# Sigmoid attention and a gated MLP: the scores' bias as a constant in the instruction

## The chip, the core and the metric

The kernel runs on one core of a Trainium2 chip. Such a core has a matrix engine (TensorE, PE in the profile; its weight loads are listed apart as PEld), three engines for elementwise work (VectorE, DVE; ScalarE, ACT; GpSimd, POOL) and SyncE (SP), which here only issues transfers. All of them run their own instruction streams in order and wait for each other through semaphores. Data moves between the device's memory (HBM), the on-chip SBUF and the matrix engine's accumulators (PSUM); 16 DMA engines carry the transfers. The metric is device time in microseconds; the kernel before takes 382.32 us (median of three runs, 382.04 to 382.57).

## What is computed

Per head, attention with a sigmoid in place of the softmax, and then an MLP over the joined heads:

```
scores = scale * matmul(q, k^T) - log(S)       # scale = 1/sqrt(64), S = 448
attn   = 1 / (1 + exp(-scores))
x      = matmul(attn, v)                       # 8 batches x 12 heads x 448 x 64, joined to 3584 x 768
h      = x @ w_in                              # 3584 x 2048
out    = (h * sigmoid(h)) @ w_out              # 3584 x 768
```

The term -log(S) = -6.1 is one number for the whole kernel. It is added inside the sigmoid's instruction on ScalarE, which computes func(scale * input + bias).

## The kernel before

**Units of scores.** The twelve heads of a batch are worked off in groups of four (`g`, three to a batch, 24 in all). A group's 448 keys are cut into seven chunks of 64, so there are 168 units `(g, ch)`. For each, `scores` (L170) issues four matmuls of 64x64 tiles (L177) that fill a PSUM tile `psc` of two banks, and one sigmoid on ScalarE (L184) that reads 128 x 896 scores from it and writes `attnT` to SBUF as float16. There are two `psc` buffers, so the scores of unit n can start when the sigmoid of unit n-2 has read its buffer. `values` (L194) multiplies `attnT` with v (L208, into two `pav` tiles) and VectorE scales the sum into `xT` (L219).

**Transposes.** Scores need q and k with the head dimension on the partitions. The first groups are transposed on PE (`pe_transpose`, L148) and copied out of PSUM by VectorE or ScalarE (L155, L138); later groups are reordered by ScalarE or VectorE (L138, L163) and transposed by DMA on SP's queue (L164).

**The MLP.** `h_unit` (L230) issues six matmuls for 128 columns of h (L236, into `ph`), a sigmoid on ScalarE (L248, into `tsig`, bias 0.0) and a product on VectorE (L249, into `gTr`). `out_set` (L289) forms two row blocks of the output with seven products in place of eight (L307, into `po`), with VectorE's sums (L315, L319 and on) and one ScalarE copy (L322, `m1`) between them, and stores them through SP's queue (L300). `ph`, `po`, `pav`, the transposes' `ptr` and the filling matmuls' `pw` share four PSUM buffers of one bank.

**What sets the order.** The order on every engine is fixed when the kernel is built, and nothing in it depends on how long an instruction takes. After the transposes of group 0 come 24 units in a loop (L535); behind each unit, a table `behind` (L510) puts filling matmuls on a dummy tile (`keep_busy`, L135), transposes of groups 1 to 3, rounds of `values`, or the first matmuls of the MLP (`begin`, behind units 21 and 23). From unit 24 on, units come in pairs, and `stretch` (L399) issues MLP steps between them up to a budget of nanoseconds written into the code (`paces`, L540).

**Loads.** POOL issues the loads of q, k, v (L78), `w_in` (L108, in four column quarters) and `w_out` (L115) in program order on one queue; they also turn float32 into float16. Each load waits for its buffer to be free and for a slot of the queue.

**The bias.** `bias_s` (L101) is a 128x1 float32 tile. VectorE fills it with -log(S) (L422); a first sigmoid on it (L423, into `warm`) makes ScalarE load its function table early; then L184 reads it as the bias operand 168 times. Small tiles take 32 bytes of each partition. `bias_s` lies at bytes 16768 to 16800, `warm` behind it, and behind that w_in, w_out and all other tiles, each at a multiple of 64 bytes.

Of the kernel before, what the change touches and what calls it, by code (L numbers as in the profile page):

```python
# [11 lines left out]
F32 = mybir.dt.float32  # L12
AF = mybir.ActivationFunctionType
# [4 lines left out]
def kernel(  # L18
# [9 lines left out]
    nc = tc.nc  # L28

    B, H, S, D = q.shape  # L30
    NT, DMODEL = out.shape
    DFF = moe_w_in.shape[1]
    P = 128
# [12 lines left out]
    QKSCALE = 1.0 / math.sqrt(D)  # L46
    NEG_LOG_S = -math.log(S)

    cpool = ctx.enter_context(tc.tile_pool(name="cpool", bufs=1))
# [48 lines left out]
        return st  # L98

    ident = cpool.tile([P, P], F16, tag="ident", name="ident")  # L100
    bias_s = cpool.tile([P, 1], F32, tag="biass", name="bias_s")  # L101
    warm = cpool.tile([P, 1], F32, tag="warm", name="warm")
    w_in_sb = cpool.tile([P, NCC, DFF], F16, tag="w_in_sb", name="w_in_sb")
    w_out_sb = cpool.tile([P, NFC, DMODEL], F16, tag="w_out_sb", name="w_out_sb")
# [63 lines left out]
    attnT = {}  # L168

    def scores(g, ch):  # L170
        attnT[g, ch] = p12.tile([P, 2, S], F16, tag="attnT", name="attnT")
        psc = ps_sc.tile([P, 2, 512], F32, tag="pssc", name="psc")
        for half in range(2):
            own = slice(half * HP, (half + 1) * HP)
            for j in range(2):
                rows = slice(j * D, (j + 1) * D)
                nc.tensor.matmul(  # L177
                    psc[own, j, :S],
                    qkT["k", g][rows, ch, own],
                    qkT["q", g][rows, :, own],  # L180
                    start=True,
                    stop=True,
                )
        nc.scalar.activation(  # L184
            attnT[g, ch], psc[:, :, :S], AF.Sigmoid, bias=bias_s, scale=QKSCALE
        )

    xT = {}
# [230 lines left out]
    load_w_in(0)  # L419

    nc.vector.memset(dummy, 0.5)
    nc.vector.memset(bias_s, NEG_LOG_S)  # L422
    nc.scalar.activation(warm, bias_s, AF.Sigmoid, bias=bias_s, scale=1.0)  # L423
    nc.vector.tensor_copy(flat["q", 0][:, :, :SPLIT], first_q[:, :, :SPLIT])
    act_copy(flat["q", 0][:, :, SPLIT:], first_q[:, :, SPLIT:])

# [108 lines left out]
    for n in range(NT_B + 3):  # L535
        scores(*units[n])
        for do, *what in behind.get(n, ()):
            do(*what)
# [3 lines left out]
    for n in range(NT_B + 3, len(units), 2):  # L542
        burst = units[n : n + 2]
        if n == 2 * NT_B:
            values_if_any()
            stretch(21500)
        for u in burst:
            scores(*u)
        values_if_any()
        rows_if_any()  # L550
        for g, ch in burst:
            if ch == NCH - 1:
                waiting.append(g)
        if n in (24, 30):
            transposes(4 + (n - 24) // 6, "k")
        elif n in (26, 32):
            transposes(4 + (n - 26) // 6, "q")
        stretch(paces[1] if 1 not in ready else paces[n // NT_B])
# [34 lines left out]
```

## Time and profile before

| | |
|---|---|
| runs, median (lowest to highest) | 382.32 us (382.04 to 382.57) |
| profiled execution, first to last instruction | 380.8 us |
| PE busy, share of the span | 372.2 us, 98% |
| ScalarE busy | 240.3 us, 63% |
| VectorE busy | 234.3 us, 62% |
| L184, 168 times | 158.9 us busy, 1010 ns each on average |
| granted TensorE clock | 0.998 on average |
| moved by DMA | 42.80 MB |

The profiled execution's own time is given as its span alone; the runs' times also hold what lies before the first and after the last instruction.

A line of the table of groups reads: source line, engine, operation, tile written<-tiles read, shapes, count | busy us in all, mean ns of one | idle time of the engine just before them, and what ended most of it. A line of the order of time reads: start and length in us, engine, line, operation, tiles, shapes, count, and in brackets the engine's idle time before it with what ended it; like instructions that follow one another are merged. In the chain that ended last, the work is followed back from the last instruction to what released each step. Matmuls overlap in the pipeline of the array, so the length of one in the profile is longer than the step from one to the next.

### The profile page before, as it was taken

The page shows a single profiled execution, that of the slowest core. Times are in us where ns is not written, and L with a number is a line of the kernel's source. Part 1 is how long each engine was busy: PE and PEld are TensorE (multiplying, and loading weights), DVE is VectorE, ACT ScalarE, POOL GpSimd, SP SyncE. Part 2 cuts the span into 40 slices and gives each one's busy share as a digit, 9 for nine tenths or more (in the row PEclk, how much of TensorE's full clock was granted, in tenths as well). Part 3 has the DMA queues.
Part 4 walks back from the last instruction along what each step waited for, and adds up shares of the span by engine and source line. Part 5 has one row for each costly group of instructions (what it writes and reads, how often), then busy time and mean ns, then how long its engine had stood idle before and what let it go on. Part 6 is the DMA issues. An engine that isn't in the chain of part 4 may idle for free.

```text
span 380.8 us, 7666 instructions
## 1 busy us (share of the span) xinstructions
PE 372.2 (98%) x3083; PEld 187.2 (49%) x3083; DVE 234.3 (62%) x416; ACT 240.3 (63%) x329; POOL 92.9 (24%) x158
## 2 busy tenths in 40 slices
PE   7999999999999999999999999999999999999995
PEld 3444445545554445444555444544455444555663
DVE  2446646996565666556767647735857446656773
ACT  4998885858777875778444686577774787044000
POOL 8856325402662323121311303101100000000000
PEclk9999999999999999999999999999999999999999
DMA  7999999994999937937939849535337300110233
GB/s 123 169 171 205 206 203 183 139 143 104 158 243 195 180 50 97 181 44 79 141 80 190 97 112 121 61 96 74 48 79 103 84 3 2 42 43 0 77 91 83
DMA packets 66403, 42.80 MB, mean 112 GB/s; under 512 B 37056, under 2 KB 62912, under 8 KB 66368
## 3 DMA queue, kind: packets, MB, share of 16 engines
q0 software_dynamic: 28032, 22.59, 43.7%
q1 hardware_dynamic: 38112, 19.41, 28.7%
q8 instruction: 24, 0.39, 0.4%
q10 hardware_dynamic: 224, 0.33, 0.3%
q14 instruction: 11, 0.09, 0.1%
HBM read 45.61 MB, written 11.01 MB: 149 GB/s over the span
## 4 chain that ended last, share of the span: by engine, by line
PE 87%; ACT 7%; DVE 3%; issue 1%; DMA 1%; POOL 1%; ACTq 0%; POOLq 0%
PE ph L236 35%; PE po L307 34%; PE psc L177 10%; PE pav L208 8%; ACT attnT L184 5%; DVE gTr L249 1%; DMA kf<-in_k_dram 1%; ACT qr L138 1%; DVE T L278 1%; PE ptrk L148 1%; ACT tsig L248 0%; POOL kf L78 0%; ACT kr L138 0%; PE ptrq L148 0%; DVE S L319 0%
## 5 line engine op out<-in xcount | busy, mean ns | idle before, releaser
L184 ACT ACTIVATE attnT<-psc,bias_s 128x896 f16<-128x896 f32 x168 | 158.9, 1010 | 53.5 <-PE psc L177 53.4
L236 PE MATMUL ph<-xT,w_in_sb 128*128 128x448 f16 x768 | 153.2, 353 | 0.0
L249 DVE TENSOR_TENSOR gTr<-ph,tsig 128x448 f16<-128x448 f32 x128 | 78.1, 623 | 72.0 <-ACT tsig L248 71.4
L236 PEld LDWEIGHTS <-w_in_sb 128*128 128x128 f16 x768 | 71.9, 98 | 75.7 <-issue 12.9
L248 ACT ACTIVATE tsig<-ph 128x448 f16<-128x448 f32 x128 | 68.2, 545 | 47.8 <-PE ph L236 46.2
L78 POOL DMA_DIRECT2D vf<-in_v_dram x48 | 28.6, 613 | 136.6 <-PE pav L208 136.3
L307 PEld LDWEIGHTS <-S 128*128 128x128 f16 x448 | 42.3, 98 | 33.9 <-issue 6.8
L315 DVE SCALAR_TENSOR_TENSOR osb<-po,osb 128x384 f32<-128x384 f32 x70 | 37.7, 555 | 25.1 <-PE po L307 24.5
L177 PE MATMUL psc<-qT,kT 64*64 64x448 f16 x672 | 50.6, 362 | 1.6 <-ACT attnT L184 1.0
L219 DVE TENSOR_SCALAR xT<-pav 128x448 f16<-128x448 f32 x48 | 27.7, 620 | 30.1 <-PE pav L208 30.1
L307 PE MATMUL po<-T,S 128*128 128x384 f16 x224 | 40.6, 327 | 0.1
L307 PEld LDWEIGHTS <-gTr 128*128 128x128 f16 x304 | 28.7, 98 | 23.4 <-issue 5.2
L307 PE MATMUL po<-w_out_sb,S 128*128 128x384 f16 x224 | 39.9, 326 | 0.0
L208 PE MATMUL pav<-attnT,vf 64*64 64x448 f16 x672 | 37.6, 349 | 0.4 <-DVE gTr L249 0.4
L78 POOL DMA_DIRECT2D qf<-in_q_dram x46 | 27.6, 610 | 41.3 <-DVE qr L163 16.9
L307 PE MATMUL po<-w_out_sb,gTr 128*128 128x384 f16 x192 | 34.7, 327 | 0.0
L78 POOL DMA_DIRECT2D kf<-in_k_dram x50 | 30.2, 615 | 7.6 <-DVE kr L163 4.4
L177 PEld LDWEIGHTS <-kT 64*64 64x64 f16 x672 | 14.9, 104 | 32.0 <-issue 30.5
L208 PEld LDWEIGHTS <-vf 64*64 64x64 f16 x672 | 20.1, 107 | 12.4 <-issue 1.8
L315 DVE SCALAR_TENSOR_TENSOR osb<-po,m 128x384 f32<-128x384 f32 x42 | 23.2, 552 | 4.1 <-PE po L307 2.5
L322 ACT ACTIVATE m<-po 128x384 f32<-128x384 f32 x14 | 6.9, 491 | 23.7 <-PE po L307 23.7
L307 PE MATMUL po<-T,gTr 128*128 128x384 f16 x112 | 21.4, 326 | 0.0
(41 smaller groups left out, 132.4 us busy)
## 6 DMA issues: line engine op xcount, KB each, us to landing
out_dram<-osb SPq DMA_DIRECT2D x54, 192.0 KB, 2.9
vf<-in_v_dram POOLq DMA_DIRECT2D x48, 112.0 KB, 4.7
kf<-in_k_dram POOLq DMA_DIRECT2D x46, 112.0 KB, 5.7
qf<-in_q_dram POOLq DMA_DIRECT2D x46, 112.0 KB, 6.0
w_in_sb<-in_moe_w_in_dram POOLq DMA_DIRECT2D x4, 768.0 KB, 10.6
w_out_sb<-in_moe_w_out_dram POOLq DMA_DIRECT2D x4, 768.0 KB, 17.4
kT<-kr SPq DMA_TRANSPOSE x18, 6.0
qT<-qr SPq DMA_TRANSPOSE x18, 5.9
```

What stands on the lines that cost most here:

```text
L78: nc.gpsimd.dma_start(flat[name, g][half * HP : (half + 1) * HP, :, c0:c1].rearrange("p i c d -> p i (c d)"), source[name][b, h0 : h0 + 2] ...
L138: nc.scalar.activation(o, i, AF.Copy)
L177: nc.tensor.matmul(psc[own, j, :S], qkT["k", g][rows, ch, own], qkT["q", g][rows, :, own], start=True, stop=True,)
L184: nc.scalar.activation(attnT[g, ch], psc[:, :, :S], AF.Sigmoid, bias=bias_s, scale=QKSCALE)
L208: nc.tensor.matmul(pav[half][j * D : (j + 1) * D, :S], flat["v", g][own, j, ch, :], at[own, j, :], start=(ch == 0), stop=(ch == NCH - 1),)
L219: nc.vector.tensor_scalar_mul(xT[b][:, half * NQ + iq, :], pav[half][:, :S], SX)
L236: nc.tensor.matmul(ph[:, :S], w_in_sb[:, cc, fc * P : (fc + 1) * P], xT[b][:, cc, :], start=(at == 0), stop=(at == NCC - 1),)
L248: nc.scalar.activation(tsig, ph[:, :S], AF.Sigmoid, bias=0.0, scale=ISX)
L249: nc.vector.tensor_mul(gTr[:, fc, (b % 2) * S : (b % 2) * S + S], ph[:, :S], tsig)
L307: nc.tensor.matmul(po[:, :NO2], a[:, fc, :], w[:, fc, :], start=(fc == 0), stop=(fc == NHC - 1))
L315: nc.vector.scalar_tensor_tensor(out=o, in0=po, scalar=sign, in1=x, op0=ALU.mult, op1=ALU.add)
L322: nc.scalar.activation(m1, po, AF.Copy, scale=ISX)
```

## The change

The tile `bias_s` and its memset are gone. L184 names the number itself as its bias, which then stands in the instruction as L248's 0.0 does. The first sigmoid now reads `warm`, which VectorE sets to zero before, and takes the same constant.

```diff
     ident = cpool.tile([P, P], F16, tag="ident", name="ident")
-    bias_s = cpool.tile([P, 1], F32, tag="biass", name="bias_s")
     warm = cpool.tile([P, 1], F32, tag="warm", name="warm")
...
         nc.scalar.activation(
-            attnT[g, ch], psc[:, :, :S], AF.Sigmoid, bias=bias_s, scale=QKSCALE
+            attnT[g, ch], psc[:, :, :S], AF.Sigmoid, bias=NEG_LOG_S, scale=QKSCALE
         )
...
     nc.vector.memset(dummy, 0.5)
-    nc.vector.memset(bias_s, NEG_LOG_S)
-    nc.scalar.activation(warm, bias_s, AF.Sigmoid, bias=bias_s, scale=1.0)
+    nc.vector.memset(warm, 0.0)
+    nc.scalar.activation(warm, warm, AF.Sigmoid, bias=NEG_LOG_S, scale=1.0)
```

## The prediction

> **What bounds the kernel now.** I read the page first, then the busy time by windows, the waits of PE, and then the order of time around the few moments at which PE stands still. From the page:
>
> ```profile
> span 380.8 us, 7666 instructions
> PE 372.2 (98%) x3083; PEld 187.2 (49%) x3083; DVE 234.3 (62%) x416; ACT 240.3 (63%) x329; POOL 92.9 (24%) x158
> ...
> PE 87%; ACT 7%; DVE 3%; issue 1%; DMA 1%; POOL 1%; ACTq 0%; POOLq 0%
> ...
> L184 ACT ACTIVATE attnT<-psc,bias_s 128x896 f16<-128x896 f32 x168 | 158.9, 1010 | 53.5 <-PE psc L177 53.4
> ...
> L248 ACT ACTIVATE tsig<-ph 128x448 f16<-128x448 f32 x128 | 68.2, 545 | 47.8 <-PE ph L236 46.2
> ...
> L322 ACT ACTIVATE m<-po 128x384 f32<-128x384 f32 x14 | 6.9, 491 | 23.7 <-PE po L307 23.7
> ```
>
> PE is busy for 98% of the span and carries 87% of the chain. The edited instruction, L184, is the largest group on ScalarE (168 of them), but ScalarE is idle 53.5 us in front of it, waiting for scores. A shorter L184 therefore counts only where PE waits for ScalarE. The windows say where that can be; the columns are window, length, PE busy (instructions), granted clock, DMA share, GB/s:
>
> ```profile
> 7.80:16.00 8.20, 7.47 (x90) 1.00 1.20 178
> 16.00:26.30 10.30, 9.42 (x163) 1.00 1.10 154
> 26.30:80.00 53.70, 53.22 (x449) 1.00 1.30 184
> 80.00:331.00 251.00, 250.52 (x2088) 1.00 0.68 103
> ```
>
> Between 26.3 and 331 us PE idles for less than 1 us. Before 26.3 us it has holes, and the DMA engines are full (share above 1). The order of time there, first ScalarE, then PE, then POOL's issues:
>
> ```profile
> 7.81 21.78 ACT L184 ACTIVATE attnT<-psc,bias_s 128x896 f16<-128x896 f32 x24 [0.80 <-PE psc L177]
> ```
>
> ```profile
> 15.92 0.58 PE L148 MATMUL ptrq<-ident,qf 128*64 128x128 f16 x14 [0.38 <-DMA qf<-in_q_dram]
> ...
> 20.24 0.58 PE L148 MATMUL ptrq<-ident,qf 128*64 128x128 f16 x14
> 20.76 0.38 PE L177 MATMUL psc<-qT,kT 64*64 64x448 f16 x4
> ...
> 24.22 0.38 PE L177 MATMUL psc<-qT,kT 64*64 64x448 f16 x4 [0.19 <-ACT attnT L184]
> ...
> 26.33 0.93 PE L236 MATMUL ph<-xT,w_in_sb 128*128 128x448 f16 x4
> ```
>
> ```profile
> 16.07 0.59 POOL L78 DMA_DIRECT2D qf<-in_q_dram  x1 [1.50 <-DMA qf<-in_q_dram]
> 16.65 0.85 POOL L108 DMA_DIRECT2D w_in_sb<-in_moe_w_in_dram  x1
> ```
>
> So for its first 24 units of scores ScalarE runs without a pause, one sigmoid every (21.78 - 1.01)/23 = 0.90 us; PE waits for it, but also for loads.
>
> **The change part by part.** *The instruction.* One immediate-bias sigmoid is in the trace: L248, 545 ns for 448 elements. With L322 (491 ns for 384, no bias) it gives (545-491)/64 = 0.84 ns an element, and a fixed part of 545-373 = 172 ns. L184 has 1007 (its median) less 896 x 0.833 = 747, that is 260. So the tile costs 88 ns and L184 should take some 918. Over 168 of them ScalarE gains 15 us, nearly all of it idle time.
>
> *Back to back.* Two instructions overlap, so what counts in a burst is the period. L184 to L184 is 0.89 at its shortest (starts at 23.11, 24.00 and 24.89 in the chain). For the immediate form this pair of L248 bounds it:
>
> ```profile
> 33.28 0.98 ACT L248 ACTIVATE tsig<-ph 128x448 f16<-128x448 f32 x2
> ```
>
> 0.98 less one duration of 0.54 is a period of 0.43, that is 0.06 above the 0.373 of streaming. For 896 elements: 0.747 + 0.06 = 0.81. The lower bound of the gain is zero (the overlap shrinks by as much as the duration), the upper 0.09; the pair is the same operation from PSUM, so I take 0.805, 0.085 less. The Trainium skill, page "ScalarE: Activation LUTs", section "What ACT_TABLE_LOAD costs", has 186 ns + 0.833 an element with immediates, 93 for each pointer operand, and an overlap of 93. By it the new period would be an estimated 0.84, and the same working gives a sum of some 0.8 instead of 1.15; the trace has a larger overlap (1.007 - 0.89 = 0.117), and it decides.
>
> *The first 26 us.* Unit n (counted from 0) has two score buffers, so its scores start 0.05 us after the sigmoid of unit n-2 ends. Up to 16 us nothing is won: unit 10's scores follow the transposes at 15.92, which wait for a load; a faster ScalarE lets PE arrive earlier and wait longer, some 0.9 us instead of 0.38. Again at 20.24: that q load was issued at 16.07 and took 4.0 us, to 20.07, and unit 15's scores at 20.76 stand behind it. From here ScalarE sets the pace. Scores are ready 0.43 after they start (45.54 to 45.97 in a later unit), so unit 15's sigmoid can start at 21.19 instead of 22.22; today ScalarE is behind by a unit. Unit 19's starts at 21.19 + 4 x 0.805 = 24.41 and ends at 25.33; unit 21's scores start at 25.38 (26.01 before), and L236 follows 0.32 later at 25.70. But L236 reads w_in, issued at 16.65 and 8.9 us on its way, so landed at 25.55; with the 0.17 that PE needed after the q load it starts at 25.72. Before: 26.33. The stage gives 0.61, bounded by 0 (w_in a little later) and by 1.0 (loads earlier).
>
> *Behind it* PE is full, and the next loads have slack: w_in's second quarter lands at 31.7 for a use at 33.3, the third at 38.9 for 42.2; w_out's last at 61.9 for a use at 63.3. So 0.61 stays.
>
> *Three later stalls.* PE waits three times for a buffer that a short ScalarE burst frees:
>
> ```profile
> 34.12 0.77 PE L148 MATMUL ptrq<-ident,qf 128*64 128x128 f16 x14
> ```
>
> ```profile
> 49.02 0.57 PE L208 MATMUL pav<-attnT,vf 64*64 64x448 f16 x8 [0.42 <-DVE gTr L249]
> ```
>
> ```profile
> 144.43 0.38 PE L177 MATMUL psc<-qT,kT 64*64 64x448 f16 x4 [0.48 <-ACT attnT L184]
> ```
>
> The first is 0.77 where others take 0.58. Before the first two, two L184 stand ahead of the tsig that DVE's gTr needs; before the third, two L184 themselves. Each burst shortens by two steps, 0.17 to 0.18, which is less than the stall. Together 0.54; between 0 and, if the stalls went whole, about 1.1.
>
> *The rest.* The memset of bias_s (0.06 us on DVE) gives way to one of warm, and the first sigmoid (294 ns) still runs long before the first data at 4.8 us: nothing, covered by the wait for the first loads. No DMA is added, and POOL, SP and the order on every engine stay. One thing moves: bias_s holds 32 bytes of each partition (16768 to 16800), and every tile allocated after it starts 32 bytes lower, at 32 past a multiple of 64 instead of on one. I cost that at nothing; the trace has no instruction to price it, and it is a rival in both directions.
>
> Sum: 0.61 + 0.54 = 1.15 us off the profiled span of 380.8, so 379.65. The median of the runs, 382.32, is 1.5 above the span, which I take as lying around it: **381.2 us**, 0.3% faster. 0.2% (0.76 us) is about what a measurement of this kernel can tell from no change.
>
> **The rivals.** *Loads eat the first stage.* For it: PE already waits for q at 15.92, and w_in's landing and the faster ScalarE meet within 0.02 us. If w_in is 0.6 late in another execution, only the three stalls are left: 381.8. Against: the runs agree within 0.5 us.
>
> *The price of the bias stays,* because the constant is kept in SBUF or the overlap shrinks: 382.3. Against it stand the 172 ns of L248, whose 0.0 is a constant of the same kind; only a special treatment of zero would speak for it.
>
> *The moved addresses cost PE time.* Place: the 1552 full-array matmuls of L236 and L307, at 189 and 163 ns a step, in stretches where PE never idles. Each ns on one is 1.55 us, so 0.75 ns undoes the gain and 1.25 ns makes it slower by over 0.2%; 2 ns give 384.3. For it: no operand in the trace lies 32 past a multiple of 64. Against: both steps are within 3 ns of streaming alone.
>
> *The moved addresses help the loads.* If transfers move whole 256-byte blocks of SBUF, a row of q, k or v (two runs of 896 bytes) touches 64 pieces of 32 bytes now and 62 then, 3% less; from 6.6 us on, q at 20.07 comes 0.4 earlier and w_in 0.6, so ScalarE's pace decides: 1.0 + 0.54, or 380.8. The Trainium skill, page "DMA: Bandwidth & Descriptors", section "How a descriptor splits into AXI transactions", says that a transaction must begin on a 256 B boundary; no row here shows whether it holds for writes.
>
> **How the numbers follow.** Forecast 0.50 (380.8 to 381.6 by its own bounds), loads eat it 0.18, price stays 0.06, addresses cost PE 0.11, loads helped 0.15. Faster by over 0.2% (below 381.56): forecast and helped loads, 0.65. Within 0.2%: 0.24. Slower: 0.11. The range leaves out the slow rival and the far end of the helped loads: 380.4 to 382.5.
>
> **What would show it.** L184 at about 918 ns; periods of 0.80 to 0.81 inside the first burst; PE's wait before the transposes near 15.9 at some 0.9 us; L236 starting near 25.7; the stall before L208 near 48 us at about 0.25, and that of L177 near 143 at about 0.3. Matmul steps of 189 and 163 that have grown, or a w_in that lands after 26 us, make the prediction wrong; so does an L184 that still takes 1007.

## The result

The changed kernel takes 381.06 us (median of seven executions, 380.42 to 381.95) against 382.57 us (382.04 to 382.69) for the kernel before on the same chip: ratio 0.9969, 95% interval 0.9958 to 0.9979. That is 1.19 us by the ratio (the two medians lie 1.51 us apart); forecast were 1.15 us and 381.2.

From the page of the profile after: the span, the engines, the chain that ended last and three groups. The wait in the row of L235 is new.

```profile
span 380.2 us, 7666 instructions
PE 370.8 (98%) x3083; PEld 186.0 (49%) x3083; DVE 235.2 (62%) x416; ACT 225.9 (59%) x329; POOL 93.5 (25%) x158
...
PE 78%; DMA 13%; POOL 3%; DVE 3%; ACT 2%; issue 1%; ACTq 0%; POOLq 0%
...
L183 ACT ACTIVATE attnT<-psc 128x896 f16<-128x896 f32 x168 | 144.2, 918 | 59.9 <-PE psc L176 59.8
L235 PE MATMUL ph<-xT,w_in_sb 128*128 128x448 f16 x768 | 153.2, 353 | 1.2 <-DMA w_in_sb<-in_moe_w_in_dram 1.2
...
L247 ACT ACTIVATE tsig<-ph 128x448 f16<-128x448 f32 x128 | 68.6, 547 | 54.4 <-PE ph L235 53.7
```

Line numbers from 101 on are one lower than before, since the tile's line is gone. The sigmoid of the scores, now L183, takes 918 ns on average where it took 1010, and ScalarE is busy for 14.4 us less, nearly all of it idle time won. ScalarE's share of the chain that ended last falls from 7% to 2%, and DMA's rises from 1% to 13%. That is the length of the loads through which this chain now runs, and not a wait of PE: PE waits 1.2 us for w_in, in the row of L235. The span of this one execution is only 0.6 us shorter; it is the slowest of the seven (381.95 us), and the experiments show what holds its first stage.

The order of time where the first stage ends, PE, kernel after:

```profile
18.12 0.58 PE L147 MATMUL ptrk<-ident,kf 128*64 128x128 f16 x14 [0.23 <-DMA kf<-in_k_dram]
...
19.28 0.58 PE L147 MATMUL ptrq<-ident,qf 128*64 128x128 f16 x14 [0.27 <-DMA qf<-in_q_dram]
...
24.50 0.38 PE L176 MATMUL psc<-qT,kT 64*64 64x448 f16 x4
26.11 0.74 PE L235 MATMUL ph<-xT,w_in_sb 128*128 128x448 f16 x3 [1.23 <-DMA w_in_sb<-in_moe_w_in_dram]
```

Unit 21's scores start at 24.50, 1.51 us earlier than before; 0.36 us of this is not the change's, since the first sigmoid of the scores starts at 7.45 here and at 7.81 before (over all profiles at 7.43 to 8.04, with the tile and without). The first h matmul behind them waits 1.23 us for w_in and starts only 0.22 us earlier (26.33 before). Loads are not all that keeps ScalarE from its shortest period of 0.797 us: between units 4 and 10 the sigmoids start 0.825 to 0.871 us apart, while PE, with transposes and filling matmuls between the scores, is busy for 7.95 of the 8.20 us from 7.8 to 16. The three stalls further on, same kernel:

```profile
33.90 0.59 PE L147 MATMUL ptrq<-ident,qf 128*64 128x128 f16 x14
```

```profile
48.44 1.29 PE L207 MATMUL pav<-attnT,vf 64*64 64x448 f16 x21 [0.24 <-DVE gTr L248]
```

```profile
143.67 0.38 PE L176 MATMUL psc<-qT,kT 64*64 64x448 f16 x4 [0.30 <-ACT attnT L183]
```

The first is gone (0.59 for the 14 transposes, 0.77 before), the second fell from 0.42 to 0.24, the third from 0.48 to 0.30. Matched matmul by matmul, the lead over the kernel before is 0.22 us at the first h matmul and 0.39, 0.58 and 0.76 us behind the three places, and from the first h matmul on it changes nowhere else up to PE's end.

### The profile page after: what moved, and what is told of

It is laid out like the page before. It is cut to its first block, busy times and chain, and to the rows that moved or that the text cites. A ratio compares the mean times of both kernels' runs of the same rounds, so it can differ in the third digit from the quotient of the medians.

```text
span 380.2 us, 7666 instructions
## 1 busy us (share of the span) xinstructions
PE 370.8 (98%) x3083; PEld 186.0 (49%) x3083; DVE 235.2 (62%) x416; ACT 225.9 (59%) x329; POOL 93.5 (25%) x158
## 4 chain that ended last, share of the span: by engine, by line
PE 78%; DMA 13%; POOL 3%; DVE 3%; ACT 2%; issue 1%; ACTq 0%; POOLq 0%
PE po L306 34%; PE ph L235 29%; PE psc L176 8%; PE pav L207 6%; DMA w_in_sb<-in_moe_w_in_dram 5%; DMA w_out_sb<-in_moe_w_out_dram 5%; DMA qf<-in_q_dram 1%; DMA vf<-in_v_dram 1%; POOL kf L78 1%; DVE gTr L248 1%; DVE T L277 1%; POOL qf L78 1%; ACT qr L137 1%; POOL vf L78 1%; ACT attnT L183 0%
## 5 line engine op out<-in xcount | busy, mean ns | idle before, releaser
L183 ACT ACTIVATE attnT<-psc 128x896 f16<-128x896 f32 x168 | 144.2, 918 | 59.9 <-PE psc L176 59.8
L235 PE MATMUL ph<-xT,w_in_sb 128*128 128x448 f16 x768 | 153.2, 353 | 1.2 <-DMA w_in_sb<-in_moe_w_in_dram 1.2
L248 DVE TENSOR_TENSOR gTr<-ph,tsig 128x448 f16<-128x448 f32 x128 | 78.9, 623 | 70.1 <-ACT tsig L247 68.6
L235 PEld LDWEIGHTS <-w_in_sb 128*128 128x128 f16 x768 | 71.9, 98 | 77.1 <-issue 12.8
L78 POOL DMA_DIRECT2D qf<-in_q_dram x46 | 27.7, 613 | 39.4 <-DVE qr L162 16.7
```

The costliest lines, as they stand in the source:

```text
L78: nc.gpsimd.dma_start(flat[name, g][half * HP : (half + 1) * HP, :, c0:c1].rearrange("p i c d -> p i (c d)"), source[name][b, h0 : h0 + 2] ...
L183: nc.scalar.activation(attnT[g, ch], psc[:, :, :S], AF.Sigmoid, bias=NEG_LOG_S, scale=QKSCALE)
L235: nc.tensor.matmul(ph[:, :S], w_in_sb[:, cc, fc * P : (fc + 1) * P], xT[b][:, cc, :], start=(at == 0), stop=(at == NCC - 1),)
L248: nc.vector.tensor_mul(gTr[:, fc, (b % 2) * S : (b % 2) * S + S], ph[:, :S], tsig)
```

## The experiments

Two questions were open: whether the shorter instruction, and not the tiles' moved addresses, makes the gain; and what holds the first stage. Ratios are to the kernel before, with 95% intervals; lines of each kernel carry its own numbers. Times of landing are from the trace's records of the transfers.

**The changed kernel with the old addresses.**

```diff
+    pad = cpool.tile([P, 1], F32, tag="pad", name="pad")
     warm = cpool.tile([P, 1], F32, tag="warm", name="warm")
...
-    nc.vector.memset(warm, 0.0)
-    nc.scalar.activation(warm, warm, AF.Sigmoid, bias=NEG_LOG_S, scale=1.0)
+    nc.vector.memset(pad, 0.0)
+    nc.scalar.activation(warm, pad, AF.Sigmoid, bias=NEG_LOG_S, scale=1.0)
```

> The constant bias as in the changed kernel, but an unused 128x1 tile stands where bias_s stood, so that every tile keeps the address it has in the kernel before. Theory (the price of the operand): L184 at 917 ns, the three late stalls shorter by 0.17 to 0.19 us each as in the changed kernel, ratio to the kernel before 0.9965 to 0.9980, as the changed kernel's 0.9969. Rival (the moved addresses are part of the effect): another ratio than the changed kernel's, by more than 0.0010 either way, and w_in's first quarter landing at 25.6 as in the kernel before instead of 26.1.

Measured: 0.9952 (0.9935 to 0.9970), medians 381.09 against 382.61. The gain is there without the move of addresses. The ratio lies below the range expected, with an interval that overlaps the changed kernel's, and the executions of the kernel before beside it reached up to 384.6 us, so a small difference from the addresses is not excluded by the times. In its profile w_in lands at 24.55, at neither of the two times that the expectation named, and the first h matmul starts at 24.90; the three late places are 0.17 to 0.18 us shorter, as in the changed kernel.

**The kernel before with the new addresses.**

```diff
+    pad = cpool.tile([P, 1], F32, tag="pad", name="pad")
     warm = cpool.tile([P, 1], F32, tag="warm", name="warm")
...
-    nc.scalar.activation(warm, bias_s, AF.Sigmoid, bias=bias_s, scale=1.0)
+    nc.vector.memset(pad, 0.0)
+    nc.scalar.activation(warm, pad, AF.Sigmoid, bias=bias_s, scale=1.0)
```

> The kernel before with the bias tile, and one more 128x1 tile, so that all later tiles lie 32 past a multiple of 64 bytes. Theory: ratio 1.000, within 0.001, L184 at 1007 ns, matmul steps 189 and 163 ns. Rival (addresses): a change of 0.2% or more either way.

The later tiles lie 32 bytes higher than in the kernel before, where the changed kernel has them 32 bytes lower; either way they stand at 32 past a multiple of 64.

Measured: 0.9993 (0.9982 to 1.0005). Two groups from its page, the scores' sigmoid and the h matmul:

```profile
L185 ACT ACTIVATE attnT<-psc,bias_s 128x896 f16<-128x896 f32 x168 | 158.9, 1016 | 53.1 <-PE psc L178 53.1
L237 PE MATMUL ph<-xT,w_in_sb 128*128 128x448 f16 x768 | 153.2, 353 | 0.0
```

The matmul group is the same to the digit as before, and the stalls are as before (0.42 and 0.48 us). Tiles at 32 past a multiple of 64 bytes cost PE nothing that these runs can tell.

**The constant in one part of the units only.** In both, the tile stays and `scores` chooses; the other kernel has `>= 24` in the condition:

```diff
-            attnT[g, ch], psc[:, :, :S], AF.Sigmoid, bias=bias_s, scale=QKSCALE
+            attnT[g, ch],
+            psc[:, :, :S],
+            AF.Sigmoid,
+            bias=NEG_LOG_S if g * NCH + ch < 24 else bias_s,
+            scale=QKSCALE,
```

> The constant in the first 24 of the 168 sigmoids only; the other 144 read the tile. Theory: only the first stage gains, up to where w_in's first quarter lands: L235's line (the first h matmul) starts 0.2 to 0.7 us earlier than in the kernel before, the stalls near 34, 48 and 143 us stay at 0.2, 0.42 and 0.48 us; ratio 0.9982 to 0.9995. Rival (the first stage is bound by loads alone): ratio 1.000.

> The constant in the last 144 sigmoids only; the first 24 read the tile. Theory: the first h matmul starts at 26.3 as in the kernel before, and the three stalls give 0.17 to 0.19 us each, 0.54 in all: ratio 0.9986, within 0.0006. Rival (all of the gain is in the first stage): ratio 1.000.

Measured: 0.9975 (0.9960 to 0.9989) for the first 24, 0.9981 (0.9969 to 0.9992) for the rest. The first gains more than its range, though the interval reaches into it; the second lies in its range. Groups of the first of the two, with both forms in one trace:

```profile
L184 ACT ACTIVATE attnT<-psc,bias_s 128x896 f16<-128x896 f32 x144 | 137.2, 1006 | 52.7 <-PE psc L177 52.6
...
L184 ACT ACTIVATE attnT<-psc 128x896 f16<-128x896 f32 x24 | 19.9, 944 | 1.9 <-PE psc L177 1.9
```

The difference of the two rows is not the operand's price, since they are of different units, and in the first burst a sigmoid is recorded longer than later. The first 24 units take 1034 to 1075 ns on average in the three profiles with the tile there and 926 to 946 in the five with the constant; the price is read from the medians of the later units, 1007 and 917.

In the profile of the kernel with the constant in the first 24 the first h matmul starts at 25.75, just behind w_in, and the whole lead of 0.57 us is made there; the late stalls keep their lengths, 0.42 and 0.48. In the other kernel the first h matmul starts at 26.48, as with the tile, and the three steps from one matmul to the next that held 0.22, 0.77 and 0.85 us with the tile hold 0.05, 0.59 and 0.67. So the gain has the two parts that the prediction named, and either is about half. The two gains add to 0.0044 where the changed kernel has 0.0031; the intervals allow for that.

**The changed kernel beside the kernels below.**

> The changed kernel once more, beside the next three on one chip. Theory: ratio 0.9969, within 0.0012. In its profile the first h matmul waits for w_in's first quarter, which lands between 25.4 and 26.2 us.

> The changed kernel beside the next two on one chip. Ratio 0.9969, within 0.0012; the first h matmul at 24.9 to 26.1, held by the loads of group 3's k and q or by w_in's first quarter; the three late stalls as in the changed kernel's profile.

Measured: 0.9969 (0.9957 to 0.9981) and 0.9982 (0.9971 to 0.9993); the executions of the latter lie between 380.47 and 382.74 us. The second ratio lies just outside its range. In the first of the two the landing of w_in was expected at 25.4 to 26.2 us, with PE waiting for it. It landed at 24.47, and the first h matmul stands so:

```profile
18.58 0.58 PE L147 MATMUL ptrk<-ident,kf 128*64 128x128 f16 x14 [0.50 <-DVE xT L218]
...
24.94 0.38 PE L176 MATMUL psc<-qT,kT 64*64 64x448 f16 x4
25.26 0.93 PE L235 MATMUL ph<-xT,w_in_sb 128*128 128x448 f16 x4
```

Here PE does not wait for w_in at all, and the span is 379.2 us. What held it was the load of group 3's k (and, behind it, VectorE's copy of kT, for which group 3's q transposes waited 0.26 us). The load landed at 18.45, 0.13 us ahead of the transposes at 18.58. (The profile names VectorE's scaling, which ended at about the same moment; in the two kernels below with group 3's loads moved forward the same transposes start ahead of that scaling's end.) In the second, w_in landed at 26.00 and PE waited 0.54 us for it.

All profiles with loads in the order and size of the kernel before and one bias operand at most, the first h matmul beside w_in's landing, in us:

| bias in the first 24 units | first h matmul | w_in landed |
|---|---|---|
| tile: kernel before | 26.33 | 25.57 |
| tile: new addresses | 26.08 | 24.32 |
| tile: constant from 24 on | 26.48 | 24.43 |
| constant: changed kernel | 26.11 | 26.06 |
| constant: changed, second | 25.26 | 24.47 |
| constant: changed, third | 26.05 | 26.00 |
| constant: old addresses | 24.90 | 24.55 |
| constant: first 24 only | 25.75 | 25.71 |

With the tile the start does not follow w_in. ScalarE sets it: the three starts lie within 0.4 us, and each 18.44 to 18.52 us behind the first sigmoid of the scores in its execution. With the constant it lies between 24.9 and 26.1, and three of five stand 0.04 to 0.05 us behind w_in. The means are 26.30 and 25.61, a gain of 0.68.

**w_in's first quarter in two halves, in the changed kernel and in the kernel before.**

```diff
     def load_w_in(step):
-        cols = slice(step * DFF // 4, (step + 1) * DFF // 4)
-        nc.gpsimd.dma_start(
-            w_in_sb[:, :, cols], moe_w_in[:, cols].rearrange("(cc p) f -> p cc f", p=P)
-        )
+        parts = 2 if step == 0 else 1
+        for part in range(parts):
+            c0 = step * DFF // 4 + part * DFF // 4 // parts
+            cols = slice(c0, c0 + DFF // 4 // parts)
+            nc.gpsimd.dma_start(
+                w_in_sb[:, :, cols], moe_w_in[:, cols].rearrange("(cc p) f -> p cc f", p=P)
+            )
```

> The changed kernel, with the first quarter of w_in loaded as two transfers of 256 columns in place of one of 512, so that what the first h matmul reads lands some 2.7 us earlier (half of the 5.5 to 6.9 us that the transfer takes). Theory (w_in's landing caps the first stage): the first h matmul starts at 24.8 to 25.0, where PE stood ready, 0.8 to 1.3 us ahead of the changed kernel; ratio to the kernel before 0.9935 to 0.9950. Rival (another load or ScalarE holds it as well): ratio 0.9969 as without the split.

> The kernel before with the same split of w_in's first quarter. Theory: ScalarE sets the pace of the first stage here (the first h matmul at 26.33 with w_in landed at 25.57), so an earlier w_in brings at most the share of executions in which it lands late: ratio 0.9990 to 1.0000. Rival (loads hold the first stage with the tile as well): ratio below 0.9980.

Measured: 0.9982 (0.9969 to 0.9996) for the changed kernel, 1.0012 (1.0000 to 1.0024) for the kernel before. The first expectation failed, and the second ratio lies above its range. The profile of the changed kernel with halves, PE:

```profile
18.53 0.58 PE L150 MATMUL ptrk<-ident,kf 128*64 128x128 f16 x14 [0.63 <-DMA kf<-in_k_dram]
...
24.92 0.38 PE L179 MATMUL psc<-qT,kT 64*64 64x448 f16 x4
25.24 0.93 PE L238 MATMUL ph<-xT,w_in_sb 128*128 128x448 f16 x4
```

The first half lands at 22.36, but the stage still ends at 25.24, held by group 3's k at 18.53 and by ScalarE's pace from there. w_in is one of two caps, not the cap. The twelve executions spread from 380.64 to 383.28 (the five of the changed kernel beside them from 380.96 to 381.96); the kernel before with halves reaches 384.33, and 383.19 without. What the additional transfer costs in those executions was not traced.

**Group 3's k and q loaded ahead of group 2's v, in both kernels.**

```diff
+    load("kq", 3)
     load("v", 2)
-    load("kq", 3)
     load_w_in(0)
```

> The changed kernel with the loads of group 3's k and q put ahead of group 2's v, so that they land some 1.2 us earlier (two loads of 0.55 to 0.6 us each), with no transfer more or less and w_in's place as it was. Theory (with the shorter sigmoid the first stage is held by the loads of group 3 and, behind them, by w_in): the waits of 0.2 to 0.6 us before group 3's transposes go, ScalarE keeps a period of 0.80 to 0.81 from unit 0 on, and the first h matmul starts when w_in has landed, at 24.3 to 24.7 in an execution in which that is early: 0.3 to 0.7 us ahead of the changed kernel, ratio 0.9950 to 0.9965. Rival (w_in alone caps the stage): ratio as the changed kernel's beside it, within 0.0006.

> The kernel before with the same change of order. Theory: ScalarE's period of 0.89 holds the first stage and no load does, so nothing is won: ratio 1.000, within 0.001, the first h matmul at 26.1 to 26.5. Rival (loads hold this stage with the tile, too): ratio below 0.9985.

Measured: 0.9972 (0.9960 to 0.9984) for the changed kernel, 1.0000 (0.9992 to 1.0009) for the kernel before. PE in the changed one, and its longest wait after the start:

```profile
17.89 0.58 PE L147 MATMUL ptrk<-ident,kf 128*64 128x128 f16 x14
18.71 0.60 PE L147 MATMUL ptrq<-ident,qf 128*64 128x128 f16 x14
25.69 0.55 PE L235 MATMUL ph<-xT,w_in_sb 128*128 128x448 f16 x2 [1.04 <-DMA w_in_sb<-in_moe_w_in_dram]
```

The waits at group 3 are gone, unit 21's scores start at 24.26, and then w_in, landed at 25.65, takes 1.04 us of it back. The expected period of 0.80 to 0.81 us throughout did not come: between units 7 and 11 the sigmoids start 0.815 to 0.825 apart, and from unit 15 to unit 16 the step is 1.10. There PE's third `values` matmul starts 0.05 us behind the end of VectorE's copy of kT. `pav` and `ptr` share their PSUM buffers, so VectorE's copies look like a third cap behind the two of the loads; no run tests this. In time this kernel and the changed kernel beside it (0.9972 and 0.9982) are not told apart, and the ratio misses its range of 0.9950 to 0.9965. The kernel before gains nothing from the same order, as expected of a stage that ScalarE paces (its first h matmul starts at 26.04).

**Both changes of the loads.** The halves and the new order together, in the changed kernel.

> The changed kernel with group 3's k and q ahead of group 2's v and w_in's first quarter as two halves. Theory (after the order of the loads, only w_in's landing is left to hold the first stage): the first half lands by 23.5, the first h matmul starts at 24.3 to 24.8 without a wait, the span is 378.5 to 378.9, and the executions lie closer together than without the halves: ratio 0.9945 to 0.9958. Rival (halving costs elsewhere what it wins, as the halved kernels so far did not gain): ratio 0.9972, as with the order of the loads alone, or above.

Measured: 0.9976 (0.9963 to 0.9989); the rival holds. The first h matmul starts at 24.31 without a wait, 2.02 us ahead of the kernel before, and 0.38 us of this comes from an earlier first sigmoid of the scores (7.43). The span is 380.3, and the executions spread from 380.51 to 383.10, no closer together than without the halves (380.32 to 382.61). In the profile most of the lead is then lost in three places, PE:

```profile
35.18 0.38 PE L210 MATMUL pav<-attnT,vf 64*64 64x448 f16 x2 [0.18 <-DMA vf<-in_v_dram]
35.73 1.51 PE L210 MATMUL pav<-attnT,vf 64*64 64x448 f16 x26 [0.17 <-DMA vf<-in_v_dram]
```

```profile
78.45 0.34 PE L309 MATMUL po<-T,S 128*128 128x384 f16 x1 [0.45 <-DVE S L321]
```

```profile
132.54 0.38 PE L179 MATMUL psc<-qT,kT 64*64 64x448 f16 x4 [0.59 <-DMA qT<-qr]
```

The first is a load and the third a transpose by DMA; why VectorE's sum comes late at the second was not traced. Matched against the kernel before, and at this kernel's own times, the lead is 2.18 us behind the stall near 32 us, 1.48 behind that at 48, 1.09 at 78, 0.33 at 133 and 0.49 at the end. A kernel that clears the first stage can run into the next loads. It need not: in the profile of the changed kernel with the old addresses a lead of 1.43 us at the first h matmul grows to 1.96 at the three late places, and nothing of it is lost.

**One operand more.** The kernel before with the scale, too, as a tile.

```diff
+    scale_s = cpool.tile([P, 1], F32, tag="scales", name="scale_s")
...
-            attnT[g, ch], psc[:, :, :S], AF.Sigmoid, bias=bias_s, scale=QKSCALE
+            attnT[g, ch], psc[:, :, :S], AF.Sigmoid, bias=bias_s, scale=scale_s
...
+    nc.vector.memset(scale_s, QKSCALE)
```

> The kernel before with its scale, too, as a 128x1 tile in place of a constant: one more operand of the kind that the change takes away. Theory: L184 takes 1007 + 88 = 1095 ns and its period 0.98; the three stalls grow by 0.17 to 0.19 us each, and the first h matmul starts 0.8 us later, at 27.1; together 1.35 us, ratio 1.0035, within 0.0010. Rival (only bursts without slack in the trace count and the growth is absorbed): ratio under 1.0015.

Measured: 1.0087 (1.0074 to 1.0100), 385.81 us. The price of the operand was right, the expected effect far too small. ScalarE's first burst, then the end of the first stage on PE, then PE's waits:

```profile
7.86 22.84 ACT L185 ACTIVATE attnT<-psc,bias_s,scale_s 128x896 f16<-128x896 f32 x23 [0.48 <-PE psc L178]
```

```profile
27.78 0.38 PE L178 MATMUL psc<-qT,kT 64*64 64x448 f16 x4 [0.23 <-ACT attnT L185]
28.10 0.93 PE L237 MATMUL ph<-xT,w_in_sb 128*128 128x448 f16 x4
```

```profile
PE psc L178 <- ACT attnT L185: 2.7, 9, 0.6
```

L185 takes 1104 ns on average (1010 before; the medians are 1097 and 1007) with a period of 0.98 (0.89 before). The first h matmul comes 1.77 us later, and not 0.8: some twenty periods of 0.09, from unit 0 on, since in this profile ScalarE's burst is not interrupted by any wait for a load. At the three stalls the lag grows by 0.18 us each, and at five further places between 58 and 312 us, where the profile of the kernel before shows no wait, by 0.09 to 0.18 each. Adding 0.09 us to the instruction costs 3.3 us by the ratio; taking 0.09 away wins 1.2. Lengthening is paid wherever a burst has no slack; shortening is won only up to what holds PE next, in the first stage a load.

## Why the prediction held

*The price of the operand: right.* 918 ns were forecast; the median is 917 in every kernel with the constant in all units, the average 918 in the changed kernel. The period in the first burst was put at 0.805 and is 0.797 at its shortest, against 0.89. The overlap of two instructions is the same in both forms (1.007 - 0.89 = 0.117 before, 0.917 - 0.797 = 0.120 after), as the pair of L248 had shown. The Trainium skill's page "ScalarE: Activation LUTs", section "What ACT_TABLE_LOAD costs", agrees on the price of the operand (93 ns there, 90 here); its overlap of 93 ns does not hold here. The smaller sum that the prediction drew from that page came from a slip: it set the page's new period (0.84) beside the measured old one (0.89), while the page's own old period would be an estimated 0.93, so that by the page, too, each step wins 93 ns.

*"Up to 16 us nothing is won": wrong.* The wait for q at 15.92 belonged to that one execution, in which q landed at 15.78; in twelve of the thirteen other profiles it landed at 14.0 to 14.6. In the changed kernel's profile it landed at 14.14, the transposes started at 14.79 without a wait, and unit 21's scores were 1.51 us ahead, or 1.15 when both are counted from the first sigmoid of the scores, not 0.63. One reading in this step was off, too: 22.22 is the start of unit 16's sigmoid. Unit 15's starts at 21.33 in the kernel before, 0.14 us behind the 21.19 of the forecast, so ScalarE is not behind by a unit there. The sum does not use the 22.22.

*The cap by w_in: right in kind, its place in time a matter of the execution.* The prediction had the first h matmul at 25.72 and the stage at 0.61, with 0 and 1.0 as bounds. Five profiles give starts from 24.90 to 26.11; against the mean of the three with the tile that is a gain of 0.19 to 1.40, on average 0.68, of which about 0.1 is an earlier first sigmoid of the scores (7.73 against 7.83 on average). The cap was a pair, w_in or the loads of group 3. The prediction had named both landings, but as one order of events with w_in last. The 0.17 us that it added behind w_in's landing are 0.04 to 0.05 where PE waits for it. And one of its signs of being wrong, a w_in that lands after 26 us, did appear: 26.06 in the profiled execution of the changed kernel, whose 381.95 us is the time that it gave to the rival of the loads (381.8). The median of the seven came out at the forecast.

*The three stalls: right.* Each is 0.17 to 0.19 us shorter by the matched leads, together 0.54 in the changed kernel (0.54 forecast), and as much in every profile with the constant from unit 24 on; in the one with the constant in the first 24 units alone they are unchanged.

*Slack behind the first stage: right for the changed kernel, with a limit.* From the first h matmul on its lead changes at the three stalls alone. In the kernel with both changes of the loads a lead of 2 us is mostly lost again. Whether that is the size of the lead or the changed loads is not shown: with the loads as they were, 1.96 us were kept.

*Sum:* 0.68 + 0.54 = 1.22 from the profiles, 1.19 from the ratio, 1.15 forecast. That the first stage came out so near its 0.61 is partly luck: two errors offset each other, since more was won on ScalarE than forecast, and loads took more of it back. Single executions lie up to 0.7 us away from the average.

*The rivals.* The loads that eat the first stage are real: in the profile of the changed kernel and in its third (26.05 in the table) they leave 0.2 to 0.3 us of the stage's gain. The price did not stay. The moved addresses cost PE nothing (the h matmuls are 353 ns and 153.2 us in both). That they help the loads, by the 256-byte rule in the Trainium skill's page "DMA: Bandwidth & Descriptors", section "How a descriptor splits into AXI transactions", is not shown: w_in landed at 24.3 to 26.1 with moved addresses and at 24.4 to 25.7 with the old, and the changed kernel with the old addresses is not slower than with the new (0.9952 and 0.9969).

## What to carry to other kernels

Price an operand from two forms of the same instruction in one trace, and count it only in the bursts where another engine waits for the last of them. A profile is one execution: a load that lands late in it can hide a gain or invent a cap, so look at the landing times of several before building a sum on one. Where a stage runs close to its loads, a shorter instruction and one longer by the same step are not worth the same.

## What the runs showed of the hardware

The same transfer, w_in's first quarter, issued between 15.0 and 16.7 us behind the same loads, landed between 24.3 and 26.1 us in the eight executions of the table, a spread of 1.7 us; the issue times do not explain it (16.27 gave 24.43, 15.70 gave 26.06). Nor do the loads ahead of it: the last of them landed at 19.15 to 20.11, and w_in followed 4.7 to 6.9 us later. It makes about half of the spread in the first h matmul with the constant: without the waits for w_in the five starts would lie within about 0.6 us in place of 1.2 (an estimate from unit 21's scores, which start at 24.50 to 25.13). What delays it is open.

A tile operand cost the same as the first and as the second, and at both lengths that the runs have: by the medians of the scores' sigmoid 90 ns for the bias (917 to 1007) and 90 for the scale (1007 to 1097), and 91 ns in the first sigmoid on one element (203 to 294). Each moved the period in a burst by 0.09 us.
